# Gate by SiLU, weight units spread over steps, the small block one group later

## The chip, the cores and the metric

The kernel runs on one core of a Trainium2 chip. The metric is the device time of one launch in microseconds. Engines: TensorE (PE) for matmuls, VectorE (DVE), ScalarE (ACT) and GpSimd (POOL) for element-wise work, and the queue of SyncE (SP), which issues most transfers. Each engine takes its instructions in the order in which they were written, and an instruction that waits holds up all behind it on its engine.

## The reference

Attention over 4 batches of 8 heads (576 positions, head dimension 64) with a learned position bias, then two feed-forward layers over 2304 tokens of 512 channels:

```python
h = x @ w_in                     # 512 -> 2048
x = (h * np.cos(h)) @ w_out      # 2048 -> 512

rms = np.sqrt(np.mean(x * x, axis=-1, keepdims=True) + 1e-06)
xn = x / rms * rms_g
g = xn @ w_gate                  # 512 -> 1536
silu = g * (1.0 / (1.0 + np.exp(-g)))
val = xn @ w_val
out = silu * val @ w_out         # 1536 -> 512
```

The change lies in the second layer, called the gated layer here, and in the end of the first.

## The kernel before, in words

Each fp32 operand of a matmul is kept as a high half (a cast on ACT) and a low half (a subtraction, mostly on POOL); `halves` writes both. A product takes three matmuls in place of one (`TERMS`).

The tokens lie in five blocks `BLKS`: 0, 1, 3 and 4 of 512 tokens, and block 2, the small one, of 256. The first layer runs in 80 items (four chunks of four hidden tiles, by the five blocks). `item_up` computes a hidden tile and its cosine, `item_down` follows two items later. In the last items the 1/rms of blocks 0 and 1 is made by a plan (`RMS_PLAN`: squares, adds, a transpose `SUM`, a Newton iteration of small operations on POOL, a transpose `BACK`, the multiplication `XN`), and `QUARTERS` says how many weight conversions go into each item.

The gated layer has 12 groups (`run_group`). Groups 0 to 5 work on blocks 0 and 1, groups 6 to 11 on blocks 3 and 4, each with one pair of hidden tiles; the two blocks and the pair's two tiles are multiplied by a scheme of seven products instead of eight, P1 to P7, for the gate (g) and for the value (v). A product is six matmuls of 512 columns. The scheme needs differences of blocks (`mix`, `fit`) and of weights. `after` empties the PSUM banks R and X, applies the gate and multiplies by the value; the results `gl` go into the output products of the next group, D0 to D7, whose sums DVE takes from three PSUM banks y into SBUF. The small block is worked on in steps S0 to S3 of groups 0 to 5, and in E0 and E1 of the group after. `ORDER` writes out the order of the steps, for PE and, since the other work is issued behind each step, for all engines.

The weights come in 64-bit form. For each piece of 128 x 512: a transfer `raw` (two buffers), an absolute value on ACT (`w_abs`, L111), four operations on DVE (`w_conv`, L122 to L128), and then `build` makes units of it: `g0 gA g1 g2` and `v0 vA v1 v2` and `o0 o1` are halves of a piece (a cast L810, a subtraction L811), `gS` and `vS` are the four subtractions in place that mix the pieces of a pair (L914), which `g1 g2` and `v1 v2` then read. Behind each step of groups 0 to 5 one unit, one or two conversions and one absolute value are issued, when their inputs have been issued and the place of the unit is free (`FREES`); `keep` stores each unit for the groups 6 to 11 as soon as it has been issued. A list `background` holds the 1/rms of blocks 3 and 4, one entry behind each step from group 1. `later2` puts the halves of the mixed blocks behind given steps.

Of the kernel before, what the change touches and what calls it, by code (L numbers as in the profile page):

```python
# [52 lines left out]
def attn_moe(tc, qd, kd, vd, smallp, lrow, ident_d, wf1, wf2, rmsg, out):  # L53
# [719 lines left out]
    QUARTERS = {-16: 2, -15: 2, -14: 2, -13: 0, -12: 2, -11: 0, -10: 1, -9: 0, -8: 2, -7: 1, -6: 2, -5: 2, -4: 0, -3: 0, -2: 0, -1: 0}  # L773
# [39 lines left out]
    def fit(b, role):  # L813
# [4 lines left out]
        for kt in range(2):  # L818
            halves(hi[:, kt], lo[:, kt], t2[kt] if role == "T2" and b == 4 else x[:, kt])
# [43 lines left out]
    for q in range(PAIRS):  # L863
        units["G"] += [(k, q) for k in ("g0 gA v0 vA gS g1 g2 vS v1 v2" if q else "g0 gA vA gS v0 vS g1 g2 v1 v2").split()]
# [19 lines left out]
    def build():  # L884
        for queue in ("GO" if units["G"] and units["G"][0][1] == 0 else "OG"):
# [8 lines left out]
            return  # L894

    def make(k, q):
# [11 lines left out]
        if k[1] == "0":  # L908
            halves(wr[k][:, 0], wr[k][:, 1], a)
            built.append((k, q))  # L910
        elif k[1] == "S":
# [377 lines left out]
```

## Time and profile before

| | us |
|---|---|
| median of 3 runs | 1217.79 (1217.46 to 1218.41) |
| the profiled execution | 1218.8 |
| its span, first to last instruction | 1216.7 |
| PE busy | 1134.0 (93%) |
| DVE busy | 914.1 (75%) |
| ACT busy | 595.3 (49%) |
| POOL busy | 536.4 (44%) |

Busy times are unions of an engine's instructions. The clock of a stretch is the share of full speed that was granted to TensorE. A wait names the instruction that waited and the one whose end released it. The groups of the gated layer are told from the trace by their first product, Rg of step gP1: group 0 begins at 702.31 us and group 6 at 1018.42 us from the span's start.

### The profile page before, as it was taken

The numbers are of one execution on the slowest core, as the hardware profiler recorded it, in microseconds if no ns is written. First come the engines' busy times: TensorE is split into PE (matmuls) and PEld (weight loads), VectorE is DVE, ScalarE is ACT, GpSimd is POOL, SyncE is SP. The second block draws the span as 40 slices with busy tenths as digits, with TensorE's granted clock in tenths as the row PEclk, the third lists the DMA queues.
The fourth block names the chain that finished last, engine by engine and source line by source line (L and its number), as shares of the span: only waits on it lengthen the run. The fifth ranks groups of instructions, "written<-read, shape, count | busy, mean of one in ns | idle before, by whom it ended". The sixth has DMA issues, their size and how long they took to land.

```text
span 1216.7 us, 18976 instructions
## 1 busy us (share of the span) xinstructions
PE 1134.0 (93%) x6748; PEld 902.1 (74%) x6748; DVE 914.1 (75%) x1661; ACT 595.3 (49%) x1199; POOL 536.4 (44%) x643
## 2 busy tenths in 40 slices
PE   9999999999999999999999886768797988999998
PEld 4577777777888888888888665646585867888886
DVE  8877988897977986986899897865675556555555
ACT  8877788876544544543554444342432433222222
POOL 0255677663423422522444668363725557111111
PEclk9999999999999999999999988888998989999999
DMA  8847475753100110111112034343444202444442
GB/s 259 265 96 208 93 209 119 207 119 63 53 35 18 50 56 18 53 53 35 35 35 71 18 135 153 111 154 104 172 157 156 70 1 72 154 156 156 156 156 87
DMA packets 54286, 131.22 MB, mean 108 GB/s; under 512 B 8912, under 2 KB 15824, under 8 KB 54192
## 3 DMA queue, kind: packets, MB, share of 16 engines
q1 hardware_dynamic: 52464, 128.26, 34.4%
q0 software_dynamic: 1584, 1.46, 0.8%
q8 instruction: 53, 0.87, 0.3%
q14 instruction: 41, 0.34, 0.1%
q10 hardware_dynamic: 144, 0.29, 0.1%
HBM read 86.06 MB, written 39.20 MB: 103 GB/s over the span
## 4 chain that ended last, share of the span: by engine, by line
PE 74%; DVE 10%; POOL 6%; ACT 4%; issue 4%; DMA 2%; POOLq 0%; DVEq 0%; ACTq 0%
PE h L626 15%; PE y L626 14%; PE y L1080 10%; PE o L326 6%; PE psS L249 6%; PE pt L286 5%; PE Rg L960 4%; PE Rv L960 4%; PE Xv L960 3%; PE Xg L960 3%; PE psb L560 2%; POOL w L914 2%; DMA raw<-in_wf_dram 2%; POOL g L811 1%; POOL wB L811 1%
## 5 line engine op out<-in xcount | busy, mean ns | idle before, releaser
L677 POOL TENSOR_TENSOR g<-t,g 128x512 fp32r<-128x512 f32 (+1 forms) x80 | 98.1, 1226 | 243.1 <-ACT g L676 243.0
L811 POOL TENSOR_TENSOR g<-t,g 128x512 fp32r<-128x512 f32 (+1 forms) x60 | 74.7, 1246 | 250.0 <-ACT g L810 231.4
L626 PE MATMUL y<-g,wB 128*128 128x512 f32 (+1 forms) x600 | 132.5, 369 | 2.0 <-DVE yaccs L711 2.0
L810 ACT CAST g<-t 128x512 fp32r<-128x512 f32 (+1 forms) x60 | 34.6, 577 | 195.6 <-DVE t L973 193.4
L1080 PE MATMUL y<-wC,g 128*128 128x512 f32 x300 | 93.3, 420 | 35.9 <-DVE yacc L995 21.2
L626 PEld LDWEIGHTS y<-g,wB 128*128 128x128 f32 x600 | 105.0, 189 | 21.6 <-DVE yaccs L711 2.4
L263 DVE CUSTOM_DVE_ANT_0 e<-psS,bias 128x576 f32<-128x576 f32 x144 | 103.4, 751 | 22.6 <-PE psS L249 20.4
L272 ACT ACTIVATE e<-e,sm 128x576 f32<-128x576 f32 x144 | 111.2, 773 | 11.3 <-DVE sm L263 11.3
L626 PE MATMUL h<-xh,wB 128*128 128x512 f32 (+1 forms) x360 | 109.3, 369 | 0.0
L671 ACT ACTIVATE r<-r 128x512 f32<-128x512 f32 (+1 forms) x80 | 47.2, 590 | 120.2 <-DVE r L668 119.9
L1080 PEld LDWEIGHTS y<-wC,g 128*128 128x128 f32 x300 | 59.9, 203 | 53.3 <-DVE yacc L995 23.8
L676 ACT CAST g<-t 128x512 fp32r<-128x512 f32 (+1 forms) x80 | 46.2, 578 | 96.0 <-DVE t L675 84.3
L1080 PE MATMUL y<-wA,g 128*128 128x512 f32 x300 | 89.9, 410 | 0.0
L995 DVE TENSOR_TENSOR yacc<-y,yacc 128x512 f32<-128x512 f32 (+1 forms) x81 | 55.1, 683 | 45.2 <-PE y L1080 44.7
L626 PE MATMUL y<-g,wC 128*128 128x512 f32 (+1 forms) x360 | 82.8, 379 | 3.8 <-ACT g L676 3.1
L326 PE MATMUL o<-eT,v 128*64 128x256 f32 (+1 forms) x640 | 84.7, 411 | 0.0
L960 PE MATMUL Rg<-xh,wB 128*128 128x512 f32 x192 | 69.7, 404 | 15.2 <-DVE r L995 15.2
L249 PE MATMUL psS<-kt,qt 64*128 64x288 f32 (+1 forms) x810 | 80.7, 309 | 0.8 <-DVE sm L263 0.7
L249 PEld LDWEIGHTS psS<-kt,qt 64*128 64x128 f32 (+1 forms) x810 | 62.5, 185 | 23.8 <-issue 9.3
L675 DVE TENSOR_TENSOR t<-r,h 128x512 f32<-128x512 f32 (+1 forms) x80 | 50.3, 629 | 35.8 <-ACT r L672 35.2
L626 PEld LDWEIGHTS y<-g,wC 128*128 128x128 f32 x360 | 64.1, 193 | 17.2 <-ACT g L676 3.5
L111 ACT ACTIVATE w<-raw 128x512 f32<-128x512 f32 x68 | 45.9, 674 | 62.6 <-DMA raw<-in_wf_dram 56.0
(197 smaller groups left out, 2896.0 us busy)
## 6 DMA issues: line engine op xcount, KB each, us to landing
raw<-in_wf_dram SPq DMA_DIRECT2D x68, 512.0 KB, 3.7
wB<-kept SPq DMA_DIRECT2D x27, 512.0 KB, 4.5
kept<-wB SPq DMA_DIRECT2D x25, 512.0 KB, 2.7
bdram<-G SPq DMA_DIRECT2D x36, 295.5 KB, 4.6
bias<-bdram SPq DMA_DIRECT2D x32, 288.0 KB, 4.2
kept<-wC SPq DMA_DIRECT2D x15, 512.0 KB, 2.6
wC<-kept SPq DMA_DIRECT2D x14, 512.0 KB, 4.6
v<-in_vd_dram SPq DMA_DIRECT2D x16, 320.0 KB, 3.4
```

The lines of the kernel that those rows point to most:

```text
L249: nc.tensor.matmul(ps[:, x, 0:288], qt[r, a, 128 * p:128 * p + 128], kt[r, b_, k0:k0 + 288], start=(n == 0), stop=(n == len(terms) - 1), t ...
L263: nc.vector.tensor_tensor_reduce(out=e.rearrange("p (a b) -> p a b", a=2), in0=ps[:, :, 0:288], in1=bias_t[j].rearrange("p (a b) -> p a b" ...
L272: nc.scalar.activation(e, e, AF.Exp, bias=s_["m"][:, j:j + 1], scale=-1.0, accum_out=s_["sum"][:, j:j + 1])
L286: nc.tensor.transpose(pt[:, 128 * i:128 * i + 128], e[:, k0:k0 + 128], ident)
L326: nc.tensor.matmul(o[64 * hh:64 * hh + 64, 0:n], vt[:, c, 64 * hh:64 * hh + 64], eT[:, 2 * c + (hh if c < 4 else 0), :], start=(c == 0), s ...
L626: nc.tensor.matmul(ps, a, b_, start=(first and k == 0), stop=(last and k == tot - 1))
L675: nc.vector.tensor_tensor(t, r, ps, op=ALU.mult)
L677: nc.gpsimd.tensor_tensor(g[:, 1, :tn], t, g[:, 0, :tn].bitcast(F32), op=ALU.subtract)
L811: (eng or nc.gpsimd).tensor_tensor(lo, x, hi.bitcast(F32), op=ALU.subtract)
L960: nc.tensor.matmul(ps, w[:, a, cols], x[b](kt), start=(start and k == 0), stop=(k == n - 1), skip_group_check=not start)
L995: nc.vector.tensor_tensor(to, x, y, op=ALU.add)
L1080: nc.tensor.matmul(y, g[a], o[:, b, cs], start=(n == 0), stop=(n == 5))
```

## The change

The gate is one activation (SiLU of the sum) where there was a sigmoid and a multiplication by the same sum on DVE. In the last chunk of the first layer the small block comes last (`LAST_CHUNK`). Its 1/rms and its halves leave the end of the first layer and group 0 for the list `background`, and its steps S stand in groups 1 to 5 and 7 instead of 0 to 5. Step vP1 stands behind the output products. Units, conversions and stores are issued by a count of ticks (two for a product, one for another step): a unit that reads a mix waits four ticks after the mix, a store four ticks after its unit, an absolute value five after its transfer; mixes go only at certain steps, and no unit of a later pair in the last six steps of a group with S. The mixes of the first pair are on POOL too. The first evictions of y are on ACT. `have` issues what a product needs and has not yet been issued. The diff, cut to its core:

```diff
+LAST_CHUNK = (0, 1, 3, 4, 2)
...
-        for bi in range(5):
+        for bi in LAST_CHUNK if c == NF1 // CH1 - 1 else range(5):
...
-        return env["psX"].tile([128, 512], F32, tag="y", name=name, bufs=3)
+        return env["psR"].tile([128, 512], F32, tag="sh", name=name, bufs=1)
...
-    QUARTERS = {-16: 2, -15: 2, -14: 2, -13: 0, -12: 2, -11: 0, -10: 1, -9: 0, -8: 2, -7: 1, -6: 2, -5: 2, -4: 0, -3: 0, -2: 0, -1: 0}
+    QUARTERS = {-16: 2, -15: 2, -14: 2, -13: 1, -12: 2, -11: 0, -10: 1, -9: 2, -8: 0, -7: 0, -6: 2, -5: 2, -4: 0, -3: 0, -2: 0, -1: 0}
     SQ, ADD, SUM, BACK, XN, OUT, MIX, FIT = range(8)
     RMS_PLAN = [
         {-14: [(SQ, 0), (SQ, 1), (ADD, 1)], -13: [(SQ, 2), (ADD, 2)], -12: [(SQ, 3), (ADD, 3)], -11: [(SUM,)], -9: [(BACK,)],
-         -8: [(XN, 0)], -7: [(XN, 1), (XN, 2), (OUT, 0)], -6: [(XN, 3), (OUT, 1)], -5: [(OUT, 2), (OUT, 3)]},
-        {-10: [(SQ, 0), (SQ, 1), (ADD, 1)], -9: [(SQ, 2), (ADD, 2)], -8: [(SQ, 3), (ADD, 3)], -7: [(SUM,)], -5: [(BACK,)],
-         -4: [(XN, 0), (XN, 1)], -3: [(XN, 2), (XN, 3)], -2: [(MIX, 0), (FIT, "B22")], -1: [(MIX, 1), (MIX, 2)]},
-        {-6: [(SQ, 0), (SQ, 1), (ADD, 1)], -5: [(SQ, 2), (ADD, 2)], -4: [(SQ, 3), (ADD, 3)], -3: [(SUM,)], -1: [(BACK,)]},
+         -8: [(XN, 0), (XN, 1)], -7: [(XN, 2), (XN, 3), (OUT, 0), (OUT, 1)], -6: [(OUT, 2), (OUT, 3)]},
+        {-10: [(SQ, 0), (SQ, 1), (ADD, 1)], -9: [(SQ, 2), (ADD, 2)], -8: [(SQ, 3), (ADD, 3)], -7: [(SUM,)], -5: [(BACK,), (XN, 0), (XN, 1)],
+         -4: [(XN, 2), (XN, 3)], -3: [(FIT, "B22")], -2: [(MIX, 0)], -1: [(MIX, 1), (MIX, 2)]},
...
+        tick[0] += 3
...
+    SHORT_IN = tuple(range(1, PAIRS)) + (PAIRS + 1,)
...
-        units["G"] += [(k, q) for k in ("g0 gA v0 vA gS g1 g2 vS v1 v2" if q else "g0 gA vA gS v0 vS g1 g2 v1 v2").split()]
+        units["G"] += [(k, q) for k in ("gA g0 gS vA v0 vS g1 g2 v1 v2" if q else "g0 gA vA gS v0 vS g1 g2 v1 v2").split()]
...
+    CLOSE = ("gP3", "S2", "gP4", "vP3", "S3", "vP4")
+    OPEN = ("vP7", "S0", "S1", "gP5", "D0", "D1", "D2", "D3", "D4", "D5", "D6", "D7", "E0", "E1")
...
+            if k[1] == "1" and k[0] != "o" and tick[0] - mixed[k[0], q] < 4:
+                continue
+            if q and (name in CLOSE or k[1] == "S" and name and name not in OPEN):
+                continue
...
-                (nc.vector if q == 0 else nc.gpsimd).tensor_tensor(to, y, z, op=op)
+                nc.gpsimd.tensor_tensor(to, y, z, op=op)
+            mixed[m, q] = tick[0]
...
-        while built:
-            k, q = built.pop(0)
+        while built and tick[0] - built[0][0] >= 4:
+            _, k, q = built.pop(0)
...
-                t = new("t")
-                nc.scalar.activation(t, c, AF.Sigmoid)
-                cur["c"], cur["t"] = c, t
+                cur["t"] = new("t")
+                nc.scalar.activation(cur["t"], c, AF.Silu)
             else:
-                silu_times(cur["t"], cur["c"], c)
+                times(cur["t"], c)
...
+    def have(p, role, unit):
+        guard = 0
+        while (unit, p) in units["G"] or (unit, p) in units["O"]:
+            guard = guard + 1
+            assert guard < 60, (p, role, unit, units["G"][:3], units["O"][:2], wstate, free)
+            if not build():
+                if needs(*units["O" if unit[0] == "o" else "G"][0])[0] < wstate["conv"]:
+                    tick[0] += 1
+                else:
+                    w_load()
+                    if wstate["conv"] == wstate["abs"]:
+                        w_abs()
+                    w_conv(1)
+                wstate["absd"], wstate["convd"] = wstate["abs"], wstate["conv"]
...
-        first, last = p % PAIRS == 0, p % PAIRS == PAIRS - 1
+        first, last = (p == SHORT_IN[0], p == SHORT_IN[-1]) if bi == 2 else (p % PAIRS == 0, p % PAIRS == PAIRS - 1)
...
-                nc.vector.tensor_copy(to, y)
+                nc.scalar.copy(to, y)
...
+    def fit_short(k):
+        y = yacc[2]
+        if k < 2:
+            for d in (2 * k, 2 * k + 1):
+                halves(xh[:, d, 2048:2304], xl[:, d, 2048:2304], y[:, d], nc.vector)
+        elif k == 2:
+            nc.vector.tensor_tensor(y[:, 2:4], y[:, 2:4], y[:, 0:2], op=ALU.subtract)
+        else:
+            halves(db[0], db[1], y[:, 2:4].rearrange("p a b -> p (a b)"), nc.vector)
...
+    for b in (2, 3, 4):
...
+                       (rms_add, b, 3), (quiet,), (quiet,), (rms_sum, b), (rms_mean, b)] + [(quiet,)] * 6 + [(rms_back, b), (quiet,)]
...
+            background += [(fit_short, k) for k in range(4)]
...
+    later2[0] = {"gP2": [(fit, 1, "T1", nc.vector)], "gP7": [(fit, 1, "T4")]}
+    later2[PAIRS - 1] = {"vP1": [(fit, 4, "B11")], "vP2": [(mix, 4, 0)], "gP6": [(fit, 4, "B21"), (mix, 4, 2)],
...
+    def steps(p):
+        down = [f"D{k}" for k in range(8)] * (p > 0) + ["E0", "E1"] * (p - 1 in SHORT_IN)
+        t = "gP1 gP2".split() + down + ["vP1"] if p else "gP1 L vP1 gP2".split()
+        t += "vP2 gP6 gP7 vP6 vP7".split()
+        if p in SHORT_IN:
+            t += "S0 S1 gP5 vP5 gP3 S2 gP4 vP3 S3 vP4".split()
+        elif p == 2 * PAIRS - 1:
+            t += "gP5 vP5 gP3 vP3 gP4 vP4".split()
+        else:
+            t += "gP5 vP5 gP3 gP4 vP3 vP4".split()
...
+    FILLS = {"gP1": 2, "vP1": 2, "gP6": 2, "vP6": 2, "gP7": 2, "vP7": 2, "gP5": 2, "gP3": 2}
...
-            if p < PAIRS:
+            if p <= PAIRS:
                 keep()
-                build()
-                w_fill(2 if p == 0 and i % 3 == 0 else 1)
-                i = wstate["abs"]
-                if i < wstate["dmad"] and i < wstate["splitd"] + NW32:
+                build(name)
+                w_fill(FILLS.get(name, 1 - int(name[1]) % 2 if name[0] in "DE" else 1) if p else 2 if i > 3 else 0)
+                x = wstate["abs"]
+                if x < wstate["dma"] and x < wstate["splitd"] + NW32 and tick[0] - asked.get(x, 0) >= 5:
...
+                if (p > 0 or i > 3) and background and not (p > 1 and background[0][0] in (rms_add, rms_xn) and name[0] in "DE" and int(name[1]) % 2 == 0) and not (
+                        p in SHORT_IN and background[0][0] in (rms_sum, rms_back) and name in ("S0", "S1", "gP5", "vP5", "gP3", "S2", "gP4", "vP3", "S3", "vP4")):
...
-    for d in range(4):
-        rms_xn(2, d)
```

## Rows read from the trace of the kernel before

**Rows 1.** The page: TensorE's busy time, and its granted clock in 40 slices.
```profile
PE 1134.0 (93%) x6748; PEld 902.1 (74%) x6748; DVE 914.1 (75%) x1661; ACT 595.3 (49%) x1199; POOL 536.4 (44%) x643
...
PEclk9999999999999999999999988888998989999999
```

**Rows 2.** Windows, one per group: length, busy PE, PEld, DVE, ACT, POOL, clock, DMA, GB/s.
```profile
692.87:702.31 9.44, 5.65 (x14) 3.98 (x13) 8.95 (x10) 4.79 (x9) 3.63 (x2) 0.67 0.14 56
702.31:746.42 44.11, 32.57 (x145) 26.68 (x144) 37.69 (x47) 22.36 (x43) 31.64 (x24) 0.88 0.40 140
746.42:813.43 67.01, 46.71 (x205) 37.70 (x204) 48.11 (x72) 24.77 (x47) 35.17 (x40) 0.85 0.39 135
813.43:864.86 51.43, 42.36 (x197) 34.16 (x196) 35.38 (x60) 16.51 (x32) 24.81 (x32) 0.93 0.36 126
864.86:915.04 50.18, 41.16 (x193) 34.16 (x192) 33.85 (x52) 18.14 (x34) 26.51 (x25) 0.90 0.46 158
915.04:965.64 50.60, 41.74 (x193) 34.55 (x192) 33.85 (x52) 18.15 (x34) 26.40 (x25) 0.90 0.39 132
965.64:1018.42 52.78, 43.49 (x193) 35.87 (x192) 28.12 (x34) 18.37 (x35) 37.48 (x31) 0.90 0.00 1
1018.42:1051.06 32.64, 32.64 (x145) 27.03 (x144) 17.39 (x26) 10.30 (x20) 10.93 (x9) 1.00 0.47 159
1051.06:1080.97 29.91, 29.91 (x133) 24.78 (x132) 15.54 (x22) 7.97 (x15) 5.19 (x4) 1.00 0.48 158
```

**Rows 3.** Waits of PE from 690 to 1020 us: total us, times, longest.
```profile
PE y L1080 <- DVE yacc L995: 21.2, 4, 7.9
PE Rg L960 <- DVE r L995: 15.2, 3, 6.6
PE y L1080 <- DVE yacc L1087: 9.8, 1, 9.8
PE rbp L758 <- POOL rsm L751: 8.4, 2, 7.2
...
PE sh L960 <- ACT xh L810: 3.6, 1, 3.6
```

**Rows 4.** Chain that ended last, 880 to 960 us: start, us, what.
```profile
908.44 1.43 PE sh L1057 x12
...
917.66 0.63 ACT wB L810
...
926.70 1.05 POOL w L914
...
927.78 0.62 ACT wC L810
...
932.15 0.61 DVE yacc L995
```

**Rows 5.** Groups by line and form, groups 3 and 4: busy, mean ns | idle before.
```profile
L811 POOL TENSOR_TENSOR g<-t,g 128x512 fp32r<-128x512 f32 x8 | 11.2, 1396 | 37.2 <-ACT g L810 37.2
...
L914 POOL TENSOR_TENSOR w<-w 128x256 f32<-128x256 f32 x9 | 8.1, 905 | 0.3
...
L122 DVE TENSOR_SCALAR w<-w 128x512 f32<-128x512 f32 x12 | 7.9, 657 | 8.8 <-ACT w L111 8.8
...
L972 DVE TENSOR_TENSOR t<-t,r 128x512 f32<-128x512 f32 x4 | 3.7, 930 | 0.0
...
L972 DVE TENSOR_TENSOR t<-t,sh 128x256 f32<-128x256 f32 x4 | 1.7, 421 | 15.9 <-ACT t L1063 15.9
```

**Rows 6.** DVE in time: one operation beside a busy POOL, and beside an idle one.
```profile
930.67 1.48 DVE L122 TENSOR_SCALAR w<-w 128x512 f32<-128x512 f32 x1
...
937.43 0.43 DVE L122 TENSOR_SCALAR w<-w 128x512 f32<-128x512 f32 x1 [0.97 <-ACT w L111]
```

**Rows 7.** Groups by line, ACT, whole span: the load of the sigmoid's table.
```profile
L1012 ACT ACT_TABLE_LOAD x1 | 1.3, 1283 | 0.0
```

**Rows 8.** POOL in time, where group 6 ends: a low half for the next group.
```profile
1051.65 1.29 POOL L811 TENSOR_TENSOR g<-t,g 128x512 fp32r<-128x512 f32 x1 [1.43 <-ACT g L810]
```

More of the change, by code (lines that the diff above doesn't have):

```diff
@@ L796, in mix @@
         if k == 0:
+            assert b == 1 or not background
             todo = [(a[:, lo], b_[:, lo], a[:, lo])]
@@ L818, in fit @@
         for kt in range(2):
-            halves(hi[:, kt], lo[:, kt], t2[kt] if role == "T2" and b == 4 else x[:, kt])
+            halves(hi[:, kt], lo[:, kt], t2[kt] if role == "T2" and b == 4 else x[:, kt], eng)
     RMS_FNS = [(rms_sq,), (rms_add,), (rms_sum, rms_mean), (rms_back,), (rms_xn,), (rms_out,), (mix,), (fit,)]
@@ L882, in needs, with build @@
         return {"A": (base + x + 1, ("a%d" % (q % 2),)), "S": (base + x + 1, ())}.get(k[1], (base + x, (k,)))
-    def build():
-        for queue in ("GO" if units["G"] and units["G"][0][1] == 0 else "OG"):
+    CLOSE = ("gP3", "S2", "gP4", "vP3", "S3", "vP4")
+    OPEN = ("vP7", "S0", "S1", "gP5", "D0", "D1", "D2", "D3", "D4", "D5", "D6", "D7", "E0", "E1")
+    def build(name=""):
+        for queue in ("G" if units["G"] and units["G"][0][1] == 0 else "OG"):
             if not units[queue]:
@@ L893, in build @@
             make(k, q)
-            return
+            return True
     def make(k, q):
@@ L988, in strassen @@
             role = m + w
+        if p < PAIRS:
+            have(p, role, m + "A" if w == "a" else role)
         product(cur[m, bank], role, c0, big(x), start)
@@ L1033, in after @@
             if m == "g":
-                gate_of_12()
-                t = new("t")
-                nc.scalar.activation(t, c, AF.Sigmoid)
-                cur["c"], cur["t"] = c, t
+                cur["t"] = new("t")
+                nc.scalar.activation(cur["t"], c, AF.Silu)
             else:
-                silu_times(cur["t"], cur["c"], c)
+                times(cur["t"], c)
                 halves(gl["21"][:, 0], gl["21"][:, 1], cur["t"])
+    def have(p, role, unit):
[12 more added lines that the diff above has]
+                wstate["absd"], wstate["convd"] = wstate["abs"], wstate["conv"]
     def short(p, k):
+        assert all(x[0] is not fit_short for x in background)
         i, m = divmod(k, 2)
@@ L1062, in short @@
             t = new("t")[:, 0:256]
-            nc.scalar.activation(t, sh[:, 0:256], AF.Sigmoid)
-            silu_times(t, sh[:, 0:256], sh[:, 256:512])
+            nc.scalar.activation(t, sh[:, 0:256], AF.Silu)
+            times(t, sh[:, 256:512])
             halves(gl["s"][:, 0, c], gl["s"][:, 1, c], t)
     def down(p, bi, d, ga_, gb_, parts=1):
-        first, last = p % PAIRS == 0, p % PAIRS == PAIRS - 1
+        first, last = (p == SHORT_IN[0], p == SHORT_IN[-1]) if bi == 2 else (p % PAIRS == 0, p % PAIRS == PAIRS - 1)
         if first and bi not in oacc:
             acc_tile(oacc, bi)
+        if p < PAIRS:
+            have(p, "o1", "o1")
         wo = [wr[x] for x in (LAST if p == 2 * PAIRS - 1 else LAST.values())]
@@ L1134, in attn_moe @@
     later2[PAIRS] = {"gP1": [(fit, 4, "T4")]}
-    FREES = {"gP3": ("g1",), "vP3": ("v1",), "vP4": ("a",), "D7": ("o0", "o1"), "E1": ("o0", "o1")}
-    FREES_SHORT = {"S0": ("g0",), "S1": ("v0",), "S2": ("g2",), "S3": ("v2",)}
-    FREES_PLAIN = {"gP2": ("g0",), "vP2": ("v0",), "gP5": ("g2",), "vP5": ("v2",)}
+    def steps(p):
[8 more added lines that the diff above has]
+            t += "gP5 vP5 gP3 gP4 vP3 vP4".split()
+        free_at = {"gP3": ("g1",), "vP3": ("v1",), "vP4": ("a",)}
+        free_at |= {"S0": ("g0",), "S1": ("v0",), "S2": ("g2",), "S3": ("v2",)} if p in SHORT_IN else {
+            "gP2": ("g0",), "vP2": ("v0",), "gP5": ("g2",), "vP5": ("v2",)}
+        if down:
+            free_at[down[-1]] = ("o0", "o1")
+        return t, free_at
+    FILLS = {"gP1": 2, "vP1": 2, "gP6": 2, "vP6": 2, "gP7": 2, "vP7": 2, "gP5": 2, "gP3": 2}
     def run_group(p):
-        kind = "first" if p == 0 else "short" if p < PAIRS else "after" if p == PAIRS else "end" if p == 2 * PAIRS - 1 else "plain"
-        frees = FREES | (FREES_SHORT if p < PAIRS else FREES_PLAIN)
-        for i, name in enumerate(ORDER[kind].split()):
+        todo, frees = steps(p)
+        for i, name in enumerate(todo):
+            tick[0] += 2 if "P" in name else 1
             if name == "L":
@@ L1174, in run_group @@
                     done(p, part_a(p) if role == "a" else role)
-                elif name == "E1" or kind in ("plain", "end"):
+                else:
                     done(p - 1, role)
@@ L1202, in attn_moe @@
     fit(1, "T2")
+    tick[0] += 2
+    build()
     fit(1, "T3")
-    for d in range(4):
-        rms_xn(2, d)
     st_psH.close()
```

45 lines of the change are left out of this document (17 added, 28 removed), and 5 rows, old and new, of the table ORDER.

## The prediction

> **What bounds the kernel now.** I read the page first: TensorE (PE) is busy 93% of the span, but its granted clock leaves full speed in the slices from about 690 to 1010 us, and only there [rows 1]. So the stretch was cut at the first product of every group of the gated layer [rows 2]. A plain group (the last row) is the yardstick: 22 products of six matmuls in 29.91 us with PE busy all the time at full clock, 1.36 us a product. Group 6, with two more products, takes 32.64 us: again nothing but PE. Groups 0 to 5 should be as full and are not. Their own work: 14 products of the two projections, 8 of the output and 2 of the small block (24 x 1.36 = 32.64), and four steps S, each 12 matmuls over 256 columns, at 1.43 us [rows 4], 38.36 us in all. Group 0 has no output products but the last down item of the layer before (12 matmuls, 2.72): 27.5 us.
>
> Loss of each group, row minus work [rows 2]: group 0 44.11 - 27.5 = 16.6; group 1 67.01 - 38.36 = 28.7; group 2 13.1; group 3 11.8; group 4 12.2; group 5 14.4; and ahead of group 0, where 9.44 us hold 14 matmuls at 0.227 = 3.2, 6.3. Together 103.1 us. The waits of PE over the stretch are mostly for DVE, five of them on y alone [rows 3]; what is lost beyond the waits is the half clock (0.90 and less in [rows 2]) that follows them.
>
> The chain tells why DVE is late in a steady group [rows 4]: ACT's cast of a weight unit (wB, later wC) stands in ACT's queue until POOL has done the four subtractions that mix that unit; behind the cast stand a sigmoid and a copy that DVE needs; DVE's queue stands, and the sums that free the y banks come last. Rows 5 have the same from DVE's side: 15.9 us in two groups before the small block's multiplication, for a sigmoid, and 8.8 us before conversions, for an ACT operation that waited for a transfer. No engine is full: DVE 33.9, POOL 26.5, ACT 18.1 of 50.2 us [rows 2]. The loss is order in queues, not work.
>
> **The change part by part.** *Steady groups 2 to 4.* Following the planner's new rules step by step: a mix is issued only at steps vP7 to gP5 or among the D steps, the unit that needs it at least four ticks later, and no unit of the next pair in the last six steps. In group 3 that puts the mix of g at gP5 and its cast at D1 of the next group, nine PE steps on; the mix of v at D0 and its cast at D4. The mix is 4 x 0.9 = 3.6 us and a low half 1.4 [rows 5]. The first cast has over 10 us of cover. The second has four D steps, 5.4 us, against about 5.7 (3.6 and the rest of a half and a unit ahead of it), but behind it stand only casts: in these groups DVE, not ACT, empties y. Both waits of [rows 4] so leave the critical queue. An Abs now comes five ticks after its transfer was issued, about 4 us in the P steps, against the 4.4 us a piece that stood before the conversions (8.8 over two groups): mostly hidden.
>
> What is late next is DVE. The gate's multiplications go: three or four of 512 at 0.93 at most and two of 256 at 0.42 [rows 5], at most 4.6 us, so 33.85 - 4.6 = 29.3 us. The same POOL work (26.5) now falls in 38.4 us instead of 50.2, a share of 0.69 instead of 0.53. An operation of DVE beside a busy POOL took 1.48 us, beside an idle one 0.43 [rows 6], and the mean of its kind was 0.66 [rows 5]: 0.23 extra at 0.53, so 0.30 at 0.69. For the 28 operations of that sort left in a group (24 conversions, 4 products) that is 2 us: 31.3 us, 82% of 38.4. Bounds for a steady group: no loss at all, or, with each of the 28 at the full 1.05 us extra, 29.3 + 28 x 0.82 = 52.3 us, more than now. I take the value nearest to the row, DVE within PE's time, and a loss of 2.5 us each for groups 3 and 4. Group 2 also holds three adds and four multiplications of 1/rms at about 0.9, some 6 us more: DVE 37.6, level with PE, so a loss of 5.
>
> The rule behind this: the Trainium skill, SBUF — State Buffer, "Who interferes with whom", says that GpSimd and VectorE share one port pair as an exclusive lock, so that the later one waits for the whole of the other's instruction. The two durations just named agree with it; by that rule alone, with POOL busy 69% of the time, every conversion could pay up to a whole POOL operation, which is the upper bound and the slower rival below.
>
> *Group 1.* Its loss of 28.7 holds the one wait of 9.8 us for the first evictions, on DVE, and one of 7.2 us for POOL's 1/rms steps [rows 3]. The first evictions go to ACT, which has one each 1.36 us and a cast of 0.62 between; the 1/rms steps are spread with six empty steps between sum and use; the transposes use the small block's bank instead of y's. Against this the small block's split (four halves on DVE and a subtraction) moves here, among conversions taken two a step. From vP1 to vP6 DVE then has about 9 us of work in five steps, 6.8 us, while POOL is busy, so it comes to gP5 some 3 to 4 us behind, and gP3, which waits for its sum one step later, 2 to 3 us late. With half clock after it and the transposes: 6. Bounds 0 and 20 (two such waits of the size of 5 to 7 us that [rows 3] has, with their half clock).
>
> *Group 0 and what is ahead.* The small block's steps S go to groups 1 to 5 and 7: no PE work is saved (4 x 1.43 + 2 x 1.36 move), and group 7, a plain group with DVE at 15.5 and POOL at 5.2 of 29.9 us [rows 2], carries them at nothing. Their wait for xh, and the sigmoid wait behind it, leave group 0. The order of blocks puts the small one last, so the last four items take less PE time, and the mixes of pair 0 move from DVE to POOL (8 x 0.9). From the item where POOL gets block 1's first operand to gP7, which needs the last of T3, POOL has nine halves at 1.4, three of 256 columns at 0.7 and the mix of v at 3.6 [rows 5]: 18.3 us. PE gets there after 14 steps of 1.36, 19.0 us (one down step of the last full block counts twice): level, 0 to 3 us of wait. DVE has 16 operations from gP2 to gP5 (eight conversions, three sums, a product, two adds, two subtractions of T1), 0.43 to 0.7 us each: 8.5 us, and with 0.30 extra each 13.3, against six products of PE, 8.2. So gP3, one product later, waits 0 to 4.5. With a half clock stretch I take 9 for both places; bounds 0 and the 22.9 of now.
>
> *Group 5.* Its wait was DVE's subtraction of the next blocks behind POOL's halves; the plan at those steps is the same but for B11, which moves from D1 to vP1, with the two halves on a POOL that has the output units there too. I keep 4 of 14.4: bounds 1 and 14.4.
>
> *Order of group boundaries, all groups from 1.* vP1 moves behind the D steps, so D0 comes one product, 1.36 us, sooner after vP4. It needs the low half of block 12: in group 6's end POOL finished it at 1051.65 + 1.29 = 1052.94 [rows 8], and D0 would be issued 2.72 us after group 7's start at 1051.06, 1053.78. It holds by 0.8 us: nothing lost. Where ACT is behind, it is lost once a group.
>
> *SiLU.* One activation for another at the same shape; the table load of 1.3 us stands once already [rows 7]. The Trainium skill, ScalarE: Activation LUTs, "Table sets: the hidden batching unit", says that functions come in named sets and a change of set costs a load; it names copies and absolute values as present in every set and not the square. By that rule the squares among the activations could cost loads, the fourth rival; the trace shows none beside the sigmoid.
>
> **Sum.** Loss left: 9 + 6 + 5 + 2.5 + 2.5 + 4 = 29 of 103.1. The profiled execution took 1218.8 us (span 1216.7): 1218.8 - 103.1 + 29 = 1144.7. The median of the runs shown is 1.0 below it, so 1144.
>
> **Rivals.**
> All hidden: DVE keeps up everywhere, a loss of 8 us remains; 1123. For it: no engine over 82%. Against: groups 0 to 2 are level by the sums above.
> DVE sets the pace: 0.7 us extra an operation instead of 0.30 makes 29.3 + 28 x 0.47 = 42.5 us a steady group, 4 over PE; with half clock some 6 in each of six groups, 1144 + 34 = 1178. For it: the single row of 1.05 extra; against: the mean of 0.23.
> Slower, the port again at its full price: if DVE's operations pay over (50.4 - 29.3) / 28 + 0.23 = 0.98 us each, a steady group is longer than now; at the 52.3 us above and the first groups as now, 1218 + 3 x 2 = 1224. Against: it needs POOL busy in front of every one.
> Silu's set lacks the square: 12 squares in groups 0 to 2, each with a load to and back, 24 x 1.3 = 31 us on ACT, of which about half would hold PE up: 1160.
> The change does not do what it says: casts meet the mix in other steps and the waits stay; 1217.
>
> **How the numbers follow.** Chances: forecast (1130 to 1162) 0.50; all hidden 0.20; DVE's pace 0.17; square 0.05; no effect 0.03; slower 0.05. Within 0.2% is what a measurement of this kernel can tell from no change. Faster 0.92, the same 0.03, slower 0.05. The range goes from just under the all-hidden case to past DVE's pace, 1122 to 1185, and leaves about 0.15 out.
>
> **What would show it.** In the profile after: no ACT cast of a weight unit with a wait for L914's mix in front of a gate's activation; DVE's wait for the small block's activation under 1 us a group; groups 3 and 4 at 38 to 41 us with the clock at 0.97 or more; no wait of y on DVE over 2 us; one table load for the gate. Waits of gP3 on DVE in groups 0 and 1 should remain. It is wrong if groups 3 and 4 stay over 45 us, if PE waits on y as long as before, or if group 7 grows by more than its 5.7 us of moved steps S.

## The result, and the profile after

The changed kernel takes 1179.93 us (median of four, 1179.42 to 1181.28) against 1218.1 (1217.46 to 1218.61): a ratio of 0.9689 [0.9672, 0.9705]. That is 38 us faster where 74 were forecast; the time lies inside the range, near its upper end, and is the one that the rival "DVE sets the pace" gave, 1178. The page has the clock back for part of the stretch only (compare [rows 1]):

```profile
PE 1123.0 (95%) x6748; PEld 893.3 (76%) x6748; DVE 874.3 (74%) x1577; ACT 606.7 (52%) x1217; POOL 539.4 (46%) x649
...
PEclk9999999999999999999999999889999999999999
```

Windows cut at the groups' first products, from group 0 to group 7, columns as in [rows 2]:

```profile
698.28:728.74 30.46, 23.74 (x100) 18.27 (x99) 23.49 (x31) 16.53 (x31) 19.91 (x16) 0.93 0.43 147
728.74:780.58 51.84, 40.13 (x183) 31.33 (x182) 38.30 (x54) 25.83 (x51) 34.01 (x39) 0.93 0.49 167
780.58:832.06 51.48, 44.44 (x201) 36.58 (x200) 39.80 (x59) 22.51 (x43) 30.61 (x37) 0.90 0.51 166
832.06:883.22 51.16, 42.35 (x201) 34.29 (x200) 39.75 (x56) 18.46 (x36) 29.30 (x36) 0.97 0.48 159
883.22:924.08 40.86, 39.05 (x193) 32.62 (x192) 30.76 (x45) 17.89 (x34) 26.84 (x24) 1.00 0.50 172
924.08:972.10 48.02, 41.03 (x193) 33.51 (x192) 29.79 (x36) 19.95 (x37) 36.75 (x28) 0.96 0.00 1
972.10:1004.74 32.64, 32.64 (x145) 27.03 (x144) 14.55 (x21) 10.49 (x20) 10.44 (x9) 1.00 0.44 143
1004.74:1040.48 35.74, 35.74 (x181) 30.52 (x180) 7.82 (x11) 14.08 (x25) 6.82 (x6) 1.00 0.40 129
```

Group 4 is what was forecast for a steady group: 40.86 us, DVE busy 30.8, clock 1.00. Groups 2 and 3, forecast at 43.4 and 40.9, take 51.5 and 51.2 with DVE busy 39.8. The span is 39.1 us shorter: 4.0 from an earlier start of group 0 (702.31 to 698.28), 42.3 in groups 0 to 5, less 7.2 that groups 6 to 11 give back (the moved steps of the small block in groups 7 and 8, 8.5, against 1.3 less in the last group).

The waits of PE from 690 to 1003 us (total, times, longest) have changed places against [rows 3]. The long ones on y and rbp are gone; what is left first is gP3's wait for the sum that DVE makes of gP5's bank, 2.9 to 5.0 us in each of groups 0 to 3 and 5:

```profile
PE Rg L974 <- DVE r L1010: 17.7, 5, 5.0
PE y L1103 <- DVE yacc L1010: 6.1, 6, 1.2
PE ssp L734 <- DVE t L986: 5.9, 2, 3.1
PE Xv L974 <- ACT wC L811: 4.9, 1, 4.9
PE y L627 <- POOL g L678: 3.8, 1, 3.8
```

The last of these stands ahead of group 0; ssp is the bank of the transposes for the sums of 1/rms, rbp that of the transposes back. Group 3 shows how that sum comes late. DVE, ACT and the DMA issues in time (start, length, instruction, idle before it and its releaser):

```profile
863.35 1.79 DVE L127 SCALAR_TENSOR_TENSOR w<-raw,w 128x512 int32<-128x512 int32 x1
865.18 1.67 DVE L129 SCALAR_TENSOR_TENSOR w<-raw,w 128x512 int32<-128x512 int32 x1
...
868.87 0.69 DVE L127 SCALAR_TENSOR_TENSOR w<-raw,w 128x512 int32<-128x512 int32 x1
...
871.76 0.43 DVE L123 TENSOR_SCALAR w<-w 128x512 f32<-128x512 f32 x1 [1.47 <-ACT w L112]
872.10 0.41 DVE L986 TENSOR_TENSOR t<-t,sh 128x256 f32<-128x256 f32 x1
...
872.76 0.68 DVE L1010 TENSOR_TENSOR r<-Rg,r 128x512 f32<-128x512 f32 x1
```

```profile
871.06 0.66 ACT L112 ACTIVATE w<-raw 128x512 f32<-128x512 f32 x1 [2.25 <-DMA raw<-in_wf_dram]
871.62 0.38 ACT L1084 ACTIVATE t<-sh 128x256 f32<-128x256 f32 x1
```

```profile
raw<-in_wf_dram SPq DMA_DIRECT2D x2, 512.0 KB, 4.0
```

Read it from the top. Two conversions take 1.7 to 1.8 us where the same one takes 0.69 later; POOL is at work beside the first two and not beside the third. The second of them is the last reader of a raw buffer; the next transfer into it takes 4.0 us and lands at about 871; ACT's Abs waits for it, the SiLU of the small block stands behind the Abs, DVE's multiplication behind that, and gP5's sum comes at 872.76. PE waits 3.48 us, and the clock is at 0.66 in the 4 us from 872.06.

### The profile page after: what moved, and what is told of

It is laid out like the page before. It is cut to its first block, busy times and chain, and to the rows that moved or that the text cites. A ratio compares the mean times of both kernels' runs of the same rounds, so it can differ in the third digit from the quotient of the medians.

```text
span 1177.6 us, 18893 instructions
## 1 busy us (share of the span) xinstructions
PE 1123.0 (95%) x6748; PEld 893.3 (76%) x6748; DVE 874.3 (74%) x1577; ACT 606.7 (52%) x1217; POOL 539.4 (46%) x649
## 5 line engine op out<-in xcount | busy, mean ns | idle before, releaser
L1103 PE MATMUL y<-wC,g 128*128 128x512 f32 x300 | 86.9, 397 | 8.6 <-DVE yacc L1010 6.1
L677 ACT CAST g<-t 128x512 fp32r<-128x512 f32 (+1 forms) x80 | 46.2, 578 | 92.4 <-DVE t L676 86.1
L974 PE MATMUL Rg<-xh,wB 128*128 128x512 f32 x192 | 71.7, 415 | 18.5 <-DVE r L1010 17.7
L1103 PE MATMUL y<-wA,g 128*128 128x512 f32 x300 | 85.1, 392 | 0.0
L1010 DVE TENSOR_TENSOR yacc<-y,yacc 128x512 f32<-128x512 f32 (+1 forms) x81 | 54.5, 682 | 35.6 <-PE y L1103 35.5
L627 PEld LDWEIGHTS y<-g,wC 128*128 128x128 f32 x360 | 63.6, 193 | 16.2 <-POOL g L678 4.0
L627 PEld LDWEIGHTS h<-xh,wB 128*128 128x128 f32 x360 | 65.8, 188 | 12.4 <-POOL wB L148 0.6
L1103 PEld LDWEIGHTS y<-wC,g 128*128 128x128 f32 x300 | 56.0, 190 | 24.1 <-DVE yacc L1010 8.6
```

Source lines behind the costliest of these rows:

```text
L627: nc.tensor.matmul(ps, a, b_, start=(first and k == 0), stop=(last and k == tot - 1))
L974: nc.tensor.matmul(ps, w[:, a, cols], x[b](kt), start=(start and k == 0), stop=(k == n - 1), skip_group_check=not start)
L1010: nc.vector.tensor_tensor(to, x, y, op=ALU.add)
L1103: nc.tensor.matmul(y, g[a], o[:, b, cs], start=(n == 0), stop=(n == 5))
```

## The experiments

Two theories were set against each other. **Amount:** DVE has too much work in groups 1 to 3, with instructions that POOL makes slow; taking work away shortens the groups by about as much. **Order:** single places in the queues hold them; moving the instruction that is waited for does it. The theories A and B in the quoted expectations are named anew for each run.

All kernels were timed beside the kernel before. The lengths are cut from the profiled execution at each group's first product, "DVE" is its busy time in groups 1 to 4 together, all in us:

| | time | g0 | g1 | g2 | g3 | g4 | g5 | g1 to g4 | DVE |
|---|---|---|---|---|---|---|---|---|---|
| before | 1218.1 | 44.1 | 67.0 | 51.4 | 50.2 | 50.6 | 52.8 | 219.2 | 151.2 |
| after | 1179.9 | 30.5 | 51.8 | 51.5 | 51.2 | 40.9 | 48.0 | 195.3 | 148.6 |
| e1 no 1/rms of 3, 4 | 1162.3 | 30.3 | 50.7 | 43.1 | 42.1 | 42.1 | 49.0 | 178.0 | 132.7 |
| e2 bank y | 1182.0 | 29.5 | 53.0 | 51.3 | 53.8 | 39.9 | 49.0 | 198.0 | 148.2 |
| e3 Abs later | 1178.3 | 31.5 | 46.6 | 52.8 | 50.3 | 44.1 | 47.8 | 193.8 | 153.1 |
| e4 sigmoid | 1195.9 | 31.2 | 55.7 | 54.2 | 53.9 | 46.1 | 50.1 | 209.9 | 161.9 |
| e5 no limit | 1169.3 | 29.4 | 50.7 | 47.3 | 49.3 | 39.5 | 48.3 | 186.8 | 137.6 |
| e6 no mix | 1162.3 | 30.4 | 47.4 | 45.6 | 47.4 | 38.6 | 47.0 | 179.0 | 141.6 |
| e7 mix 4 later | 1176.8 | 30.2 | 51.6 | 53.0 | 49.5 | 41.0 | 46.2 | 195.1 | 148.6 |
| e8 before + SiLU | 1204.7 | 43.1 | 62.4 | 52.6 | 47.8 | 47.8 | 49.2 | 210.6 | 138.0 |
| e9 gate behind gP5 | 1181.4 | 30.4 | 50.2 | 54.5 | 51.5 | 40.4 | 48.9 | 196.6 | 148.1 |
| e10 e9 + e7 + sums at D0 | 1175.0 | 30.4 | 49.1 | 53.7 | 49.9 | 40.2 | 46.3 | 192.9 | 145.5 |
| e11 e7 + sums on PE | 1175.1 | 29.7 | 50.3 | 49.8 | 51.7 | 42.3 | 46.3 | 194.1 | 140.2 |
| e12 e10 + two edits | 1170.8 | 30.2 | 46.2 | 48.7 | 50.9 | 42.9 | 46.3 | 188.6 | 143.8 |

One group alone is not exact: e7 issues the same order as the changed kernel up to group 5, and its groups 2 and 3 differ by +1.5 and -1.6. Their sum agrees to 0.2.

### e1: the 1/rms of blocks 3 and 4 left out

```diff
-    for b in (2, 3, 4):
+    for b in (2,):
```

> The changed kernel without the 1/rms of blocks 3 and 4 (their part of the background list is left out). Theory A (waits: an absolute value on ACT waits for a weight buffer that POOL's low half frees, a conversion on DVE waits behind it, and the 1/rms work comes on top): groups 2 and 3 fall from 51.5 and 51.2 us to about group 4's 40.9, group 1 by 2 to 4, so 1180 falls by 22 to 25, to about 1156. Theory B (the background costs nothing; the order of units makes groups 2 and 3 long): no group changes by more than 2 us, 1177 to 1180.

Measured 1162.34 us, ratio 0.9544 [0.953, 0.9559]: 17.6 us less than the changed kernel, short of the 1155 to 1158 of one theory and far from the 1177 to 1180 of the other; group 1 fell by 1.2 only, of the 2 to 4 forecast, but lost only 0.7 us of DVE's work. Groups 2 and 3 become steady groups:

```profile
779.14:822.25 43.11, 40.37 (x193) 33.84 (x192) 30.92 (x45) 20.02 (x38) 27.72 (x25) 0.96 0.56 189
822.25:864.36 42.11, 39.55 (x193) 32.47 (x192) 32.09 (x47) 18.01 (x34) 26.81 (x24) 1.00 0.55 188
```

DVE loses 8.9 and 7.7 us of work in them, and they are 8.4 and 9.1 us shorter: about a microsecond for a microsecond. The edit takes ACT's squares and PE's transposes away too, and with them PE's waits of 5.9 us for ssp; so this run alone does not part DVE's work from those.

### e2 and e3: two waits moved

e2 gives the transposes the y banks again, e3 holds Abs back until its buffer has been released for six ticks:

```diff
-        return env["psR"].tile([128, 512], F32, tag="sh", name=name, bufs=1)
+        return env["psX"].tile([128, 512], F32, tag="y", name=name, bufs=3)
```
```diff
-tick[0] - asked.get(x, 0) >= 5:
+tick[0] - asked.get(x, 0) >= 5 and tick[0] - released_at.get(x - NW32, -99) >= 6:
```

> The transposes of 1/rms write into the y banks again, as before the change, instead of the small block's bank. PE waits 1.4, 3.1 and 2.8 us for DVE to read that bank. Theory A (the shared bank costs these waits and some of what follows): 6 to 9 us off, 1171 to 1174. Theory B (the wait moves to the y banks, which DVE empties late): 1178 to 1183.

> An absolute value is issued at least six ticks after the unit that frees its buffer; in groups 1 to 4 it moves from the first D steps to D7 or later. Theory A (the wait for the buffer stalls ACT and DVE): DVE's idle time in the D steps (8.5, 3.5, 3.5, 2.5 us in groups 1 to 4) goes, PE's waits for sums at gP3 shrink, 1180 falls by 10 to 20, to 1160 to 1170. Theory B (DVE simply has too much work beside a busy POOL): the same work lands later, 1176 to 1184.

e2: 1182.03 us, 0.9702 [0.9688, 0.9717]. e3: 1178.29 us, 0.9675 [0.9659, 0.9691]. In e3 group 1 falls by 5.2 us and groups 2 and 4 grow by 1.3 and 3.2: what was put off came later. DVE's waits for Abs in groups 1 to 4, 28.8 us in the changed kernel, are all but gone in e3:

```profile
DVE w L123 <- ACT w L112: 2.5, 3, 1.0
```

Even so the four groups are only 1.6 us shorter: DVE's work grew by 4.5, and it waits elsewhere. In neither run did the moved wait give its time back: both speak against order.

### e4 and e8: the SiLU alone, from either side

e4 takes the sigmoid and its multiplication back into the changed kernel; e8 puts the SiLU alone into the kernel before.

```diff
-nc.scalar.activation(cur["t"], c, AF.Silu)
+nc.scalar.activation(cur["t"], c, AF.Sigmoid)
...
+times(cur["t"], cur["c"])
 times(cur["t"], c)
```

> The changed kernel with the gate as before, a sigmoid and a multiplication by the sum on DVE, at the places of before. 4 more multiplications of 512 and 2 of 256 a group on DVE, up to 4.6 us. Theory A (DVE is late in groups 0 to 3 and 5): 2 to 4 us more in each of them, 1180 rises to 1188 to 1200. Theory B (the multiplications were hidden): within 2 us of 1180.

> The kernel before with the gate's activation alone changed: SiLU in place of the sigmoid and its multiplication, all order as before. In the changed kernel the same edit undone cost 16 us. Theory A (it saves DVE's time wherever it stands): 14 to 18 us less than before, 1200 to 1204. Theory B (in the order of before, waits on POOL's queue set the groups, so that DVE's saving falls into them): 0 to 6 us less, 1212 to 1218. A gain well above 18 would mean that the order is worth less than 20 by itself.

e4: 1195.87 us, 0.9824 [0.981, 0.9839]; e8: 1204.69 us, 0.9893 [0.9876, 0.9909]. The SiLU is worth 15.9 us in the new order and 13.5 in the old, a little under e8's forecast; the order alone is worth about 22. e4 is also e1 in reverse: 13.3 us more DVE work in groups 1 to 4, 14.6 us more length, with no place of the order changed. Group 4, which had lost 2.5 us only and which theory A did not name, grew the most, by 5.3 us for 4.7 of DVE's work:

```profile
893.33:939.46 46.13, 41.07 (x192) 33.63 (x192) 35.50 (x53) 17.89 (x35) 27.17 (x24) 0.96 0.43 149
```

### e5: a quarter of the conversion left out

```diff
-            if wstate["half"] == 0:
+            if wstate["half"] == 0 and i >= 2 * NF1 + 6:
+                pass
+            elif wstate["half"] == 0:
```

> The changed kernel without one of the four conversion instructions (the limit of the magnitudes, L123) for the 30 weight pieces of pairs 1 to 5; these values are not limited, and nothing else moves. It takes 6 instructions of about 0.65 us each off DVE in every one of groups 0 to 4, some 3.6 to 4 us a group, and leaves ACT, POOL and the order alone. Theory A (DVE's work sets the pace of groups 1 to 3): groups 1, 2 and 3 each fall by 3 to 5 us from 51.8, 51.5 and 51.2, group 4 (DVE busy 30.8 of 40.9) by under 1; time 1165 to 1170. Theory B (a wait at a place in the order sets it, and DVE has idle time in each group that the work can fall into): groups 1 to 3 keep their lengths within 1.5 us; time 1176 to 1180.

1169.25 us, 0.9598 [0.9584, 0.9612]: theory A's time, for amount. The limit was 15.5 us of DVE in groups 1 to 4; the busy time fell by 11.0 only, since others took longer (L129 rose from 1025 to 1093 ns), and the four groups together by 8.5. Of groups 1 to 3, for which 3 to 5 us each were forecast, only group 2 did so (-4.2); group 3 fell by 1.8 and group 1 by 1.2, where DVE's work fell by 3.0 and 1.8.

### e6: POOL's mixes left out

```diff
-            for to, y, z, op in ((b[:, hi], b[:, lo], b[:, hi], ALU.add), ...
+            for to, y, z, op in () if q else ((b[:, hi], b[:, lo], b[:, hi], ALU.add), ...
```

> The changed kernel without the four POOL subtractions of each weight unit (L927) for pairs 1 to 5, so that 40 instructions of about 0.85 us, 34 us, leave POOL in groups 0 to 4 (the weights of these pairs are then not combined, which is left out of the computation); DVE's and ACT's instructions stay. Theory A1 (DVE is slow because POOL works beside it): DVE's busy time in groups 2 and 3 falls by 2 to 4 us from 39.8, the conversions' means from 0.55 to 1.1 us towards 0.5 to 0.7, and groups 1 to 4 become 2 to 4 us shorter each; time 1165 to 1171. Theory A2 (DVE's load counts, not its neighbour): DVE's busy time in groups 2 and 3 stays within 1 us, the groups too; time 1176 to 1180. A shorter queue on POOL alone, without shorter DVE instructions, would show as less waiting of ACT's Abs and no shorter group, as when that wait was moved.

1162.27 us, 0.9544 [0.953, 0.9559], more than A1 asked. Waits for Abs, of ACT and of DVE, over the whole span (all of them stand in groups 1 to 4), first in the changed kernel:

```profile
ACT w L112 <- POOL wB L812: 22.4, 6, 6.6
DVE w L123 <- ACT w L112: 28.8, 13, 8.5
```

and in e6:

```profile
ACT w L112 <- POOL wB L812: 8.2, 5, 3.4
DVE w L123 <- ACT w L112: 16.2, 12, 2.5
```

DVE's instructions became faster, as A1 says, but by 7.0 us of the 16.4 that groups 1 to 4 lost; the rest is idle time of DVE (46.7 to 37.4), in which the waits behind an Abs fell by 12.6 (the Abs waits until POOL gives a buffer back). That speaks against the last sentence of the expectation, but does not refute it: the queue did not become shorter by itself here. POOL's work may count twice, as a neighbour and as a queue ahead of the buffer; against the second stands e3, where the waits for Abs went and the groups stayed. How the 16.4 divides was not told apart further.

### e7: group 5

```diff
-"vP7": [(fit, 4, "T2")], "S1": [(mix, 4, 1), (fit, 4, "T3")],
+"vP7": [(fit, 4, "T2")], "gP3": [(mix, 4, 1), (fit, 4, "T3")],
```

> The changed kernel with two steps of group 5, the mix of block 4's lower half (one DVE subtraction of 1024 columns, 2.3 to 3.4 us) and the two-part split of T3, moved from step S1 behind step gP3, so that they no longer stand ahead of gP5's sum in DVE's queue. Theory A (group 5 loses its time where PE waits at gP3 for that sum, 5.05 us): group 5 falls from 48.0 to 43 to 44.5; time 1175 to 1177. Theory B (the work lands ahead of a later sum instead): group 5 stays within 1 us and the wait turns up at gP4 or vP4; time 1179 to 1181.

1176.83 us, 0.9664 [0.965, 0.9679]. The time is theory A's, but group 5 fell by 1.8 and not by the 3.5 to 5 that it rests on, and at gP3 a wait of 2.8 to 3.2 us is left (as in e10 to e12); undecided.

### e9 and e10: gP5's sum freed from what stood ahead of it

```diff
+            if i == 0:
+                pending.append(finish)       # SiLU, times, halves of S1: run behind gP5's sum
...
-tick[0] - asked.get(x, 0) >= 5:
+tick[0] - asked.get(x, 0) >= 5 and name not in ("S0", "S1"):
```

> The changed kernel with nothing left out and two edits of order ahead of PE's wait at gP3: the small block's gate of step S1 (ACT's SiLU, DVE's multiplication, the split) is issued behind gP5's sum instead of ahead of it, and no Abs of a weight piece is issued at S0 or S1 (there ACT waited 2.25 us for the piece's DMA in group 3, with the SiLU behind it, DVE's multiplication behind that, and gP5's sum behind that). In the changed kernel PE waits 3.28, 3.00, 2.90 and 3.48 us there in groups 0 to 3, and the granted clock is low right after. Theory A (the order of DVE's queue at this place costs it; DVE has room elsewhere in the group): the four waits fall to under 1 us, groups 0 to 3 each lose 3 to 5 us; time 1162 to 1169. Theory B (DVE with its slow instructions is behind in these groups, so the same work ends up ahead of another of PE's reads, as when the other waits were moved): the waits at gP3 shrink, others grow in the same groups; time 1174 to 1182.

> The kernel of e9 with two more edits of order: the mix of block 4's lower half and the split of T3 behind gP3 (as in e7), and the transposes for the sums of blocks 3 and 4 not before the first D step (PE waited 3.07 and 2.79 us for their bank at gP1 of groups 2 and 3). Theory A: on top of e9 another 2 to 3 us in group 5 and 3 to 5 us each in groups 2 and 3; time 1152 to 1161. Theory B: only group 5's 2 to 3 us stay; time 1171 to 1179.

e9: 1181.35 us, 0.9693 [0.9677, 0.9709]: no gain, as theory B had it. It is no clean test, though: in group 3 an Abs that waits 2.40 us for its transfer still stands ahead of gP5's sum, with two conversions behind it, so the hold did not reach it, and PE's wait at gP3 stayed at 3.41 us. In group 1 the edit did work: the wait of 3.0 us at gP3 went, and the group fell by 1.6, as much as one group varies by. In group 2 that wait grew from 2.9 to 3.8, and the sum of 17.7 us became 15.5:

```profile
PE Rg L974 <- DVE r L1010: 15.5, 4, 5.0
PE ssp L734 <- DVE t L986: 6.1, 2, 3.9
```

So the small block's gate was not what kept gP5's sum in group 3, and group 2 lost (+3.0) more than group 1 gained. e10: 1175.03 us, 0.9642 [0.9627, 0.9656], theory B's time (1171 to 1179), not A's (1152 to 1161): the waits for ssp went, and waits on y for DVE's sums, up to 2.6 us, came in groups 2 and 3.

### e11: less of DVE's work, with nothing left out

```diff
+        for x in (d, d + 1):
+            for k in range(4):
+                nc.tensor.matmul(rst[bi][:, 4 * x + k:4 * x + k + 1], rst[bi, x][:, 128 * k:128 * k + 128], env["one"], start=True, stop=True)
```

> The kernel of e7 with less work on DVE for 1/rms of blocks 3 and 4, all of it still computed: the three additions of squares (863 ns each) and the sum over 512 columns become 16 one-column products of PE against a column of ones, of which DVE sums 16 columns; and the four multiplications by 1/rms read it from the transposes' bank and not from a copy in SBUF (an instruction that reads PSUM took 0.68 us beside a busy POOL in this trace, one on SBUF alone 0.74 to 0.85). It takes some 7 us off DVE in groups 1 to 3, of 129.9. Theory A (DVE's work sets the pace of these groups; in e5, 14 us less on DVE made 10.7 us): 5 to 7 us less than e7's 1176.8; 1169 to 1173. Theory B (groups 1 to 3 are set by the order): 1175 to 1179. If PE's small products wait for ACT's squares or PE loses more than it gains: above 1179.

1175.05 us, 0.9642 [0.9629, 0.9655]: a miss by 2 us for A, and inside theory B's range. Against e7, DVE's work in groups 1 to 4 did fall by 8.4 us, but PE's rose by 6.0 (168.35 to 174.32, sums of the windows), for the one-column products are not small. Those products in e11, and the transposes (of blocks 3 and 4) that stood there in the changed kernel:

```profile
L743 PE MATMUL ssp<-evenm,sq 128*128 128x1 f32 x64 | 10.5, 295 | 5.6 <-DVE t L999 5.6
```
```profile
L734 PE MATMUL ssp<-ident,sq 128*128 128x128 f32 x8 | 1.8, 361 | 5.9 <-DVE t L986 5.9
```

The forecast had counted them at nothing on PE; the work changed engines, to the one that is the bound. That this ate the gain is argued: no run has the products without the rest.

### e12: the fastest with nothing left out

The Abs of e3 for group 1 alone, and 1/rms read from the transposes' bank:

```diff
+ ... and (p != 1 or tick[0] - released_at.get(x - NW32, -99) >= 6):
...
+        rst[bi] = ps[:, :tn]
+        if env["psX"] is not None:
+            return
```

> The kernel of e10 with two more edits, nothing left out: in group 1 alone, Abs at least 6 ticks behind the release of its w32 buffer (in e3, where this held in all groups, group 1 fell by 5.2 us and groups 2 and 4 grew by 1.3 and 3.2), and the multiplications by 1/rms of blocks 2 to 4 read it from the transposes' bank, which takes three copies off ACT and some 1 us off DVE. Theory A (the losses of group 1 are its own; the later groups keep the lengths they have in e10): group 1 falls from 49.1 to 44 to 46, the rest by 1 us in all; 1169 to 1172. Theory B (DVE is behind from group 1 to group 3, and what group 1 puts off is done in group 2 or 3): groups 1 to 3 together within 2 us of e10's 152.7; 1173 to 1176.

1170.84 us (1166.09 to 1171.75), 0.9606 [0.9589, 0.9624]: theory A's time, and faster than both kernels (the changed one has 0.9689 [0.9672, 0.9705]).

```profile
727.52:773.70 46.18, 40.13 (x183) 32.46 (x182) 33.82 (x48) 25.09 (x49) 33.23 (x39) 0.93 0.50 177
773.70:822.39 48.69, 43.54 (x201) 34.91 (x200) 39.92 (x60) 21.86 (x41) 30.20 (x36) 0.93 0.53 173
822.39:873.26 50.87, 42.84 (x201) 33.73 (x200) 38.31 (x58) 18.77 (x36) 29.12 (x38) 0.97 0.51 166
873.26:916.14 42.88, 39.97 (x193) 32.39 (x192) 31.79 (x48) 17.99 (x34) 27.26 (x25) 1.00 0.49 172
```

Group 1 fell by 2.9 against e10, and group 2, which theory A left alone, by 5.0; group 4 grew by 2.7. So the time came out as forecast, but not the split between the groups. Against e10 the four groups lost 4.3 us with only 1.6 less of DVE's work, so the two edits gave something beyond DVE's work; which of them did was not told apart. Groups 2 and 3 still stand at 49 to 51 us with DVE at 38 to 40: order has not mended them.

## Why the prediction was off

The loss left, term by term, each length less the work that the prediction gave it (35.64 in group 1, which has no E now; 20.4 in group 0):

| term | forecast | measured |
|---|---|---|
| ahead of group 0, and group 0 | 9 | 0.9 + 10.1 |
| group 1 | 6 | 16.2 |
| group 2 | 5 | 13.1 |
| group 3 | 2.5 | 12.8 |
| group 4 | 2.5 | 2.5 |
| group 5 | 4 | 9.7 |
| sum | 29 | 65.3 |

Ahead of group 0 the loss was 6.3; group 0 begins 4.0 us earlier with 1.4 us more of PE's work ahead of it (its down item has 256 columns now, not 512), which leaves 0.9. The sum closes: 103.1 less 65.3 is 37.8, and 1.3 from the last group make the 39.1 us of the span. The forecast's own span, 1130 to 1162, was missed. That the time lies in the range is luck: the range reached up past the rival "DVE sets the pace", whose price did not come true.

- **What bounds the kernel: right.** Groups 6 and 7 are nothing but PE (32.64 and 35.74, the latter 5.8 longer against the 5.7 forecast).
- **Waits in queues: right for the steady group.** The wait of ACT's cast for the mix in front of a gate is gone in group 4 ([rows 4]; two casts with such a wait are left, 1.0 us in group 1 and 3.2 in group 5), no wait of y on DVE is over 1.2 us, and group 4 came out to the tenth in length, with DVE's busy time (31.3 forecast, 30.8 measured) and the clock close to it.
- **The price of POOL beside DVE: right.** 0.30 us extra was taken; in groups 1 to 4 L123, L125, L127 and L129 have means of 0.62, 0.66, 0.94 and 1.03 us against 0.42, 0.42, 0.69 and 0.69 for those with POOL idle, 0.26 extra on average. The rival that gave the right time wanted 0.7 an operation and the same loss in every group, so its mechanism was not what happened.
- **Group 3 as a steady group: wrong.** The sum "2.5 each for groups 3 and 4" overlooked that the background list carries the 1/rms of block 4 through group 3 (its sum behind gP1, the last multiplication behind vP2). DVE has 39.75 us there, not 31.3. e1 takes that away, and the group loses 9.1 us.
- **"DVE 37.6, level with PE, so a loss of 5": the step that failed.** DVE's time was nearly right (39.8); what it costs was not. In groups 1 to 4 DVE stood 46.7 us beside 148.6 of work:

```profile
L123 DVE TENSOR_SCALAR w<-w 128x512 f32<-128x512 f32 x25 | 15.5, 622 | 28.8 <-ACT w L112 28.8
```
```profile
DVE t L986 <- ACT t L1084: 8.4, 4, 2.3
```

28.8 us of it stand ahead of a conversion for an Abs, which the forecast called mostly hidden, and 8.4 ahead of the small block's multiplication, which it had at under 1 us a group. It had looked at the wait of an Abs for its transfer. That fell from 47.3 to 8.6 us in these groups, but the wait for POOL to free the buffer rose from 6.3 to 22.4; first before, then after:

```profile
ACT w L111 <- DMA raw<-in_wf_dram: 47.3, 11, 9.9
ACT w L111 <- POOL wC L811: 5.2, 4, 1.8
ACT w L111 <- POOL wB L811: 1.1, 3, 0.4
```
```profile
ACT w L112 <- POOL wB L812: 22.4, 6, 6.6
ACT w L112 <- DMA raw<-in_wf_dram: 8.6, 6, 2.3
```

So the surplus counts before it reaches PE's time: e1, e4 and e5 moved the length of groups 1 to 4 by -17.3, +14.6 and -8.5 for -15.9, +13.3 and -11.0 of DVE, about one for one. The edits of order e2, e3, e7 and e9 moved it by -1.6 to +2.7. The table of the runs shows the same in another way. Length less DVE's work is the time that DVE stands: 68.0 before, 46.7 after, and 44.8 to 49.8 in the runs of the new order but e3 (40.6), e6 (37.4) and e11 (53.9). The new order took idle time out; what is left of it changed little, and the work comes on top. It is no law: in e3, e6 and e11 the length did not follow DVE's work alone.

- **Group 1: 6 forecast, 16.2 measured.** gP3's wait was forecast at 2 to 3 and is 3.0; the 4.9 us at vP7 for ACT's cast of a unit were not seen. The cast stood behind another that waited for DVE's multiplication, and DVE was late because an Abs had waited for POOL:

```profile
749.30 0.68 ACT L112 ACTIVATE w<-raw 128x512 f32<-128x512 f32 x1 [4.71 <-POOL wB L812]
```
```profile
750.01 0.79 DVE L123 TENSOR_SCALAR w<-w 128x512 f32<-128x512 f32 x1 [8.48 <-ACT w L112]
```
```profile
756.41 0.62 ACT L811 CAST g<-t 128x512 fp32r<-128x512 f32 x1 [3.39 <-DVE t L986]
```

Here order counts beside amount. As far as one group can tell, it followed DVE's work (e1 -1.2 for -0.7, e5 -1.2 for -1.8, e4 +3.8 for +3.5), and it also followed the place of Abs (e3 -5.2, for -2.5 of DVE's work) and POOL's load (e6 -4.4).

- **Group 5: too hopeful.** The mix of block 4 on DVE, kept ahead of gP5's sum, cost 5.05 us at gP3; moved (e7), only 1.8 of it came back.
- **SiLU's table: right.** One load stands before the gate, of 1283 ns as in [rows 7], and none around the squares, so that rival is out. Its worth of 15.9 us (e4) is DVE's work, as above.

What stays open: how much of the loss of groups 2 and 3 is DVE's slow instructions and how much its waiting for POOL's buffers (e6 took both away; e3 took most of the waiting away and left the groups as long, with more work on DVE). More than the six buffers that these pieces have would be a test; that was not tried.

## What to carry to other kernels

When waits are taken out of an engine's queue, add its busy time to the waits that are left in it before comparing it with the bound: at 74 to 78% of a group DVE here cost about a microsecond for a microsecond. To see whether an order or an amount holds a stretch, take a little work away and move a little work; if only the first shortens it, leave the order. And go through a background list to its end: what it puts into a group is part of that group's sum.

## What the runs showed of the hardware

- DVE's instructions with all operands in SBUF took longer beside a busy POOL, those that read PSUM did not. Counted over groups 1 to 4 of the changed kernel: L127 685 ns with POOL idle (14) and 1426 with POOL busy for over nine tenths of them (9); the sums L1010, one operand in PSUM, 679 (11) and 681 (20). The idle ones had POOL busy for under a twentieth. The Trainium skill, SBUF — State Buffer, "Who interferes with whom", says that a DVE instruction with at most one SBUF input, outside the two-port modes, does not contend with GpSimd; these counts agree. e12's use of it, 1/rms read from PSUM, took the multiplications of 512 columns from 795 ns (groups 0 to 5 of the changed kernel) to 735.
- An fp32 product with a single column stands in the trace of e11 as two matmuls of 295 ns on average: 32 of them kept PE busy for 10.5 us, the eight transposes that they replaced for 1.8.
